# Four operand transposes of an attention block moved from TensorE to the DMA queue, three norms moved to TensorE, and a new order table

## The chip, the cores and the metric

One NeuronCore of a Trainium2 chip runs the whole program. The metric is the time of one execution in microseconds (us) of device time; lower is better.

## The reference

Three blocks follow each other. `q`, `k` and `v` have 2 batches, 8 heads, 768 rows and 64 columns.

```
q_bits, k_bits = (q @ proj > 0), (k @ proj > 0)        # 6 bits each
mask   = bucket(q_bits) == bucket(k_bits)
scores = where(mask, q @ k.T / 8, -1e9)
attn   = softmax(scores);  x = attn @ v                # -> 1536 tokens x 512
h      = max(x @ w1, x @ w2, x @ w3);  x1 = h @ w_out  # d_ff 768
g      = elu(x1 @ w_in);  out = g @ w_out2             # d_ff 2048
```

## The kernel before, in words

Everything is float32 outside and split inside into pairs of float16 numbers (a high and a low part), so that each product is three float16 matmuls.

The attention is cut into 6 chunks of 256 query rows (3 per batch), each chunk into 4 head pairs (a unit, u = 0 to 23), each unit into 4 tiles of 128 query rows of one head (t = 0 to 95). For a tile TensorE makes 8 score matmuls into PSUM ring `s` (2 buffers, L621), VectorE takes the row maximum (L624) and two small factors (L625, L627), ScalarE the exponential (L629). In the units of the first chunk (u < 4) the probabilities stay float32: TensorE turns them in the same `s` buffer (L641), they are copied to SBUF (L645), and TensorE multiplies with v (L650). From u = 4 on they are split into two float16 parts (L658 or L660, then L664) and turned by a DMA (`PT<-hl`, L666), before 18 matmuls with v (L672 to L674).

`plan_qk` prepares k for each head pair (u = 0 to 3 and 12 to 15: 12 blocks of 128x128) and q for each two pairs of a chunk (every even u: 8 blocks). Its steps are: load (L388), a norm, two small instructions that make a power of two out of it (L318, L320), scaling (L396 on ScalarE or L397 on VectorE), the high part (L398, VectorE), the low part (L400, GpSimd or VectorE), transposes of the pairs on TensorE into a PSUM buffer `mo` (L410, for k in two groups of six) with a copy to `ka` or `qa` by ScalarE or VectorE (L413), a DMA that moves one half to `kb` or `qb` (L417), the projection for the bits (L429 or L431), the bits (L441), their transposition (L445, L453 to L457) and small DMAs that put them behind the halves (L464). The scores of a unit wait for all of that.

The norm is made in one of two ways. `square` has ScalarE square and sum (L333, an ACTIVATE and a read of the accumulator), `gram` has TensorE multiply each 128x128 block of upper bfloat16 halves with itself (L297) and VectorE take the maximum (L301). Both end in two matmuls with one column (L280, L281). Before the change `gram` serves q of u = 0 and k of u = 0 and 1.

Beside the first tiles the weights of the second block are converted (`dc2w`, `w`; L531 to L560), and v is (L492 to L502). The second block's matmuls (L713) begin when the first chunk is finished; the third block (L713 with `win`, L848) fills the second half of the time.

The order of the work is not made by a loop: each operation is put into a list with the engines that could do it, and the table `ORDER`, a compressed string, names for each place which operation is emitted there, and on which engine. Each engine works its instructions off in that order, so that one that waits holds up all behind it on its engine. DMAs are issued from SyncE's queue (SP) or ScalarE's (ACT). Engine letters in the table are PE, V (VectorE), A (ScalarE), G (GpSimd), D (SP).

Of the kernel before, what the change touches and what calls it, by code (L numbers as in the profile page):

```python
# [30 lines left out]
class Graph:  # L31
# [73 lines left out]
    "c-lQyOITXx))u_6@y5m*8*gm9vC$at$|h<6O~OWvfLG8cV48~QKx_wMG7y`A*bKyzf!Gejb|AI`@pK@z1F;>5?LbTiVmlB|2I9#;Ob3#a|9Sqk&H4Yezi)l-`>uDb4UgNcWz6SqKV$!(5=mvVN=j#N"  # L105
    "UYZxbaC_pfyb0VH#K#-Q{hL!L@yD)|EQI>ufz@F1o3Y)KSzPaUb6yn;&OCQ6#%A5uPUiA=F1Li6?m6)kt}A@s`|GDDxx3zQy0__k`*)Pktj44}ISg~}>3gp*<Qw!iGxo@|sC-`@Q!JXP_>nHIxOP*_"
    "Roys4;5BgO2-XzyrGa()oa>XK<R4~Lxc8|EI}ljad@;UnBlI%6^yj&H^Wo2!Qu8#Vo)4?^$Ajj`nQkc>NxwSwYa@oM^Xr)5<jv$~%S=CJet`#PhOHjtEoUn5s|h=ro!;|W@x8w$dEq%b?pO%!FK+mj"
    "jf9(3>+yuV&Mn`%EOrszj_*Z&R52#^FqUg;o{R3!U?F@3f8jFCi@%xwT^e?~E`Ih{CB%yjw?`r;HWya+13O+)9Xi;FD%7^{*}KR~Dzc`~z0$Q`gmw)Rp)0fPa^eU3kMZ}D_9eH>G2==2O1Y#N_D(NQ"
    "{-3qR1fAm-<E+zVUNIRQJF5tSPPn6-#a_?GyKM}!e7MHlfvrioIT+fb7@H?ZU;;hWJ?C4mt+orZpp1;$ncFtw<+JpFSRDMFm<%bcClb6`T6JbmVE&tOIQ7WV(BJ3^3sVZe4L;_e;zK$1Lmh4ttHao-"
    "?r68UmJ`Jd5!Ibqk(n2qpcb^!_PJO{WD|xB&z72xH_uRW#4X{!u*Rp5W&E4f8O9g07oIP#7ffC+xv8jq=kr^acNEcp?ZA$IKzVx}bx8c%OI$vGqMMu}V&*?wYf|r}L+&<DM?P$L3|k4#^*LqdKUC`Y"  # L110
    "{DrS$g0ZmfUqt+i+(2&}^Bu$z74DgD#;K##F{AER+s2=p>|=v#-C~b8u$?yx*XB~+p`P)I`60@6ZT@PlKKlANwu2oEBH@2du+YeN=Letr&-wlUH;DYAeSWkWGf3WFGxwJni70YLoJ;WqvPvm8Cs;jG"
    "u9Nyp<;=gltn?Wl6^ifdeu*02vV!7uJ}P)A(XeJqi3u4z0^vneY%W~2oeerJS9F}c=>N=zH>AIj2xYE4vu<PW7XQGVE{q5WKln*m?V!@Fx3x#tf+}KW)lk>zF?oNSQ^n-I!*lP1ukA;FLhM4ecN}+r"
    "rRr2O77w)J2KFoD^|fuAnH1JU%zr7OcE|1l#nmNr8e*1$;32YfJ@qwOhHbDI<Hu7z;j`!3H}8?nIrO{8DHpzNU?Q*`3|c-HXvLQXGr^YDJr}LTIkM#=Wq^0}x;d!F(2!bcJrPXcx~i>X$(eyvp4jRa"
    "?c#sQm~Ot=bB<3Kl(UKJ-m~x3Z^hAtS*iB#tr*vK&M-Vnm}Y#4O}*L~CMPdDf8oSmFzhn61Djp=fd5X^uDTX2PM7?Lr*5xlL352TeLd@b>t5TijdieWN71ykxlK>!>%lGmJa)ueuf@6B$G9R;y&Q=6"
    "ep4*`b?6Tkm=glgnCHM-7Sd|0val^;bg^cLZ^CtRzRk<%?>jNc-uGOk{67?5_f=e$q*XD-5t+^SD)gu2h4x5fus>CE-<;}H)V8s7))ZJ-Fld6WywheZv}S&c=t?KX7mgE7BGu98GIBM(_(eQ68<E<k"
    "#N?TBaR#L@caLz@BQ`9$PnW$O-bVEAt@G%Vv#xnLcI?@Zc)ZVizMh>IyK!cGkM$dlV*A=@gW2jhy>#L`zZ^xUeiE}yJFaWH)pl)XeEEmsvi8p0@5JswobeLj3jTSF%tzLJ{=hZk5Yc7-u@a7Oc?cd|"
# [53 lines left out]
TR = lambda blocks: (0, 625, 142 * blocks)  # L170
# [803 lines left out]
```

## Time and profile before

| | |
|---|---|
| median of 3 runs | 646.44 us (646.3 to 650.33) |
| the profiled execution's own time | 646.06 us |
| its span, first to last instruction | 644.3 us |
| TensorE busy | 624.7 us (97%) |
| VectorE busy | 528.0 us (82%) |
| ScalarE busy | 454.8 us (71%) |
| GpSimd busy | 218.5 us (34%) |

A time is one execution on the chip. The span lies inside it; 1.76 us of the profiled execution are around it. Busy is the union of the instructions of an engine. Engines overlap, so shares do not add up, and a share is a mean over stages that have different limits.

### The profile page before, as it was taken

To read this page: it belongs to the slowest core of one execution; us is meant where nothing else is said; L and a number is where in the kernel's file an instruction comes from. 1 tells how busy PE (TensorE), PEld (TensorE's weight loads), DVE (VectorE), ACT (ScalarE), POOL (GpSimd) and SP (SyncE) were. 2 spreads that over 40 slices of the span, in tenths; PEclk is the share of its full clock that TensorE was granted. 3 is DMA by queue.
4 is the path that set the end of the run, shared out by engine and by line. 5 is a ranking of instruction groups with operands and counts; after the bars stand their busy time and mean duration, and the time that the engine had idled before them with its cause. 6 is when DMAs were issued, how large, how long until landed. Compare 5 with 4: busy or idle time off the path is not lost.

```text
span 644.3 us, 16489 instructions
## 1 busy us (share of the span) xinstructions
PE 624.7 (97%) x6414; PEld 490.8 (76%) x6414; DVE 528.0 (82%) x1493; ACT 454.8 (71%) x858; POOL 218.5 (34%) x196
## 2 busy tenths in 40 slices
PE   4999889999999999999999999999999999999997
PEld 4788768888888888888888887766676666667664
DVE  6899999998878988898765898888888676887564
ACT  3899999999878777866635878866755665554431
POOL 1210175756656474575631101112111221120021
PEclk9999989999999999999999999999999999999999
DMA  8775699979799777888666634231302100000022
GB/s 261 200 242 152 180 202 229 217 131 218 150 189 178 149 156 164 174 169 151 147 132 218 181 96 128 68 99 35 97 19 71 45 1 2 1 1 2 1 92 105
DMA packets 176030, 81.35 MB, mean 126 GB/s; under 512 B 142672, under 2 KB 170320, under 8 KB 175952
## 3 DMA queue, kind: packets, MB, share of 16 engines
q1 hardware_dynamic: 171678, 75.54, 50.3%
q10 hardware_dynamic: 4274, 4.76, 2.6%
q8 instruction: 50, 0.82, 0.6%
q14 instruction: 28, 0.23, 0.1%
HBM read 38.80 MB, written 3.15 MB: 65 GB/s over the span
## 4 chain that ended last, share of the span: by engine, by line
PE 80%; DVE 4%; ACT 4%; DMA 3%; issue 1%; POOL 0%; DVEq 0%; SPq 0%; ACTq 0%
PE mo L713 47%; PE out L848 19%; PE s L621 6%; PE o L672 2%; PE o L673 2%; PE o L674 2%; ACT P L629 1%; DVE m L624 1%; DMA kb<-ka 1%; DMA rawv<-in_v_dram 1%; PE mo L410 1%; DMA PT<-hl 1%; ACT hl L645 1%; DVE hx L734 0%; ACT mo L535 0%
## 5 line engine op out<-in xcount | busy, mean ns | idle before, releaser
L713 PE MATMUL mo<-xT,w 128*128 128x256 f16 x1296 | 152.6, 272 | 0.0
L664 POOL TENSOR_TENSOR hl<-P,hl 128x768 f16<-128x768 f32 x69 | 115.0, 1674 | 64.9 <-ACT hl L658 31.5
L713 PEld LDWEIGHTS <-w 128*128 128x128 f16 x1296 | 123.6, 98 | 16.7
L713 PE MATMUL mo<-x1T,win 128*128 128x256 f16 x1152 | 135.8, 273 | 0.0
L848 PE MATMUL out<-wo2t,gt 128*128 128x512 f16 x576 | 134.9, 379 | 0.0
L713 PEld LDWEIGHTS <-win 128*128 128x128 f16 x1152 | 112.3, 98 | 24.2
L629 ACT ACTIVATE P<-s,bias,scale 128x768 f32<-128x768 f32 x96 | 94.6, 991 | 28.8 <-DVE bias L627 17.6
L841 POOL TENSOR_TENSOR gt<-g,gt 128x256 f16<-128x256 f32 x57 | 39.3, 695 | 213.2 <-ACT gt L839 125.4
L624 DVE TENSOR_REDUCE m<-s 128x1 f32<-128x768 f32 x96 | 91.1, 951 | 12.6 <-PE s L621 11.2
L848 PEld LDWEIGHTS <-gt 128*128 128x128 f16 x576 | 54.9, 97 | 52.7
L832 ACT ACTIVATE r<-mo,nih 128x256 f32<-128x256 f32 x96 | 44.8, 469 | 69.1 <-PE mo L713 65.0
L835 DVE TENSOR_SCALAR uu<-e,sg 128x256 f32<-128x256 f32 x96 | 35.5, 371 | 26.3 <-ACT e L834 25.7
L658 ACT CAST hl<-P 128x768 f16<-128x768 f32 x62 | 50.7, 830 | 2.9 <-DMA PT<-hl 2.4
L672 PE MATMUL o<-vt,PT 128*128 128x65 f16 x480 | 51.3, 193 | 0.2
L673 PE MATMUL o<-vt,PT 128*128 128x64 f16 x480 | 51.3, 194 | 0.0
L674 PE MATMUL o<-vt,PT 128*128 128x65 f16 x480 | 51.1, 192 | 0.0
L837 DVE SCALAR_TENSOR_TENSOR g<-mo,aj,uu 128x256 f32<-128x256 f32 x96 | 46.1, 482 | 6.0 <-POOL gt L841 2.0
L621 PE MATMUL s<-ka,qa 128*128 128x384 f16 x192 | 48.1, 332 | 2.5 <-ACT P L629 1.9
L621 PE MATMUL s<-kb,qb 76*128 76x384 f16 x192 | 48.2, 332 | 1.0 <-DMA kb<-ka 1.0
L672 PEld LDWEIGHTS <-PT 128*128 128x128 f16 x480 | 44.4, 96 | 2.7 <-DMA PT<-hl 0.4
L673 PEld LDWEIGHTS <-PT 128*128 128x128 f16 x480 | 44.3, 97 | 2.1
L713 PEld LDWEIGHTS <-wot 128*128 128x128 f16 x432 | 41.4, 98 | 5.6
(212 smaller groups left out, 1158.7 us busy)
## 6 DMA issues: line engine op xcount, KB each, us to landing
raww<-in_moe_w_dram SPq DMA_DIRECT2D x17, 512.0 KB
raw<-in_moe_w_in_dram SPq DMA_DIRECT2D x14, 512.0 KB
raw<-in_moe_w_out_dram SPq DMA_DIRECT2D x13, 512.0 KB
rawk<-in_k_dram SPq DMA_DIRECT2D x8, 384.0 KB
raww<-in_moe_w_out_dram SPq DMA_DIRECT2D x6, 512.0 KB
out_dram<-ot SPq DMA_DIRECT2D x12, 256.0 KB
rawq<-in_q_dram SPq DMA_DIRECT2D x10, 256.0 KB
wot<-in_v_dram SPq DMA_DIRECT2D x4, 384.0 KB
```

The costliest lines, as they stand in the source:

```text
L621: PE.matmul(ps.ap[:, h, :NK], lh[0:n, h0 + i, j], rh[0:n, i, h * CH:(h + 1) * CH], start=first, stop=not first)
L624: op({"V": vred(S)}, lambda e: V.tensor_reduce(out=m.ap, in_=ps.ap[:, :, :NK], op=ALU.max, axis=AX.XY), rd=[ps], wr=[m], prio=t + 80.5)
L629: op({"A": act(S, ap=2, acc=int(u < FU)) - 42}, lambda e: A.activation(out=P.ap.rearrange("p (c n) -> p c n", c=2), in_=ps.ap[:, :, :NK], ...
L658: A.copy(hl.ap[:, 0], P.ap)
L664: op({"G": gtt(S), "V": (vtt(S), -109.46)}, lambda e: eng[e].tensor_tensor(out=hl.ap[:, 1], in0=P.ap, in1=hl.ap[:, 0], op=ALU.subtract), r ...
L672: PE.matmul(oo, pt.ap[:, kt], vt.ap[:, i, kt, :D + 1], start=(kt == 0), stop=False)
L673: PE.matmul(oo[:, :D], pt.ap[:, kt], vt.ap[:, i, kt, D + 2:], start=False, stop=False)
L674: PE.matmul(oo, pt.ap[:, NS + kt], vt.ap[:, i, kt, :D + 1], start=False, stop=(kt == NS - 1))
L713: PE.matmul(o, lh(kk, x), rh(kk, y), start=(kk == 0 and pi == 0), stop=(kk == n - 1 and pi == 2))
L832: op({"A": act(NQ, ap=1) - 42}, lambda e, m=m, o=o, r=r: A.activation(out=r.ap, in_=o.ap[:, :NQ], func=AF.Relu, scale=nih.ap[:, m:m + 1]), ...
L837: op({"V": vstt(NQ)}, lambda e, m=m, o=o, uu=uu, gg=gg: V.scalar_tensor_tensor(out=gg.ap, in0=o.ap[:, :NQ], scalar=aj.ap[:, m:m + 1], in1= ...
L848: PE.matmul(outs[j].ap, gt.ap[:, x, j * 128:(j + 1) * 128], wo2t[f].ap[:, y], start=(len(seen) == 1 and pi == 0), stop=(len(seen) == n and ...
```

## The change

For `0 < u < 4` (k of u = 1, 2 and 3, and q of u = 2) one DMA issued from SP turns all blocks, from `nat` straight into `ka` or `qa`. The TensorE transposes and the copies out of PSUM fall away there. For all `u < 4` the norm is made by `gram`; new to it are k of u = 2 and 3 and q of u = 2. Two estimates of a DMA cost on the ACT queue are one higher in the list, which no instruction shows. `ORDER` is replaced.

```diff
 ORDER = (
...
-        x2 = norm2([(raw, fl)], N, prio, u < 1.007, acc, True, [s, inv])
+        x2 = norm2([(raw, fl)], N, prio, u < 4, acc, True, [s, inv])
...
         nb_ = nt // 2 if nt > 8 else nt
-        for c in range(nt // nb_):
+        if 0 < u < 4:
+            op({"D": TR(nt)}, lambda e: SP.dma_start_transpose(out=ta.ap.rearrange("p h s t -> p (h s) t"), in_=nat.ap.rearrange("p n t d -> p (n t d)")),
+               rd=[nat], wr=[ta, tb, bits], prio=prio)
+        for c in range(nt // nb_ if not 0 < u < 4 else 0):
             ps = mo()
```

The two tables unpack to lists of 3359 and 3352 places. Read as lists, they stand so (the number is the place):

```
                                        old place        new place
scores of tile 0, PE                    108              106
exponential of tile 0, A                126              128
exponential of tile 21, A               529              516
first matmul of the second block, PE    539              540
k u=1: transposes | DMA transpose       80, 88 PE        101 D
       bits matmul, PE                  122              122
q u=2: transposes | DMA transpose       101 PE           118 D
       bits matmul, PE                  185              169
k u=2: transposes | DMA transpose       154, 179 PE      176 D
       bits matmul, PE                  189              198
k u=3: transposes | DMA transpose       231, 254 PE      282 D
       bits matmul, PE                  275              312
       half to kb, D                    367              331
       scores of tile 12, PE            390              381
low parts (L400): k u=1, q u=2, G       63, 90           69, 116
places on PE, V, A, G, D                694 1488 776 181 218   690 1508 775 155 222
```

Between the exponentials of tile 0 and of tile 21 ScalarE has 90 places in the old list and 85 in the new one. Kind by kind the new list has there: three `square`s of k fewer and one of q more (k's are that of u = 3, which `gram` makes now, and those of u = 13 and 14, which come later; q's is that of u = 10, which comes earlier); two scalings of k (L396) more and one of q more; three copies to `ka` (L413) fewer; two casts L658 fewer; and one L535 more, one L539 and one turn of k's bits (L457) fewer. Ahead of tile 0 it has one `square` of k and one of q, one copy to `ka` and one to `qa` and one write of v fewer, one scaling of q and two conversions (L539, L543) more, and two loads of v there in place of one weight load. A load of q (for u = 4) is issued from ScalarE's queue at place 123, behind the `square`s and ahead of k's scaling (126) and tile 0's exponential; it waits until the low part of q u=2 (place 116) has been made, for the buffer.

Between the maxima of tiles 0 and 21 VectorE has 178 and 174 places. The new list has there: two scalings of k and one of q (L397) fewer, one copy to `ka` fewer, two L546 and one L560 fewer, one L502 fewer, one write of v fewer; and one each more of L436, L441, L455, a turn of k's bits, and L660. Ahead of tile 0 it has three L301 more, for the new `gram`s (one behind the scores of tile 0 in the list, all ahead of its maximum), one write of v and one L546 more, and one copy to `ka`, one scaling of q and two conversions fewer.

On SP the new DMA transposes have behind them: k u=1: two weight loads; q u=2: `kb<-ka` of k u=1 and a load of v; k u=2: a load of k for the second batch and one of weights; k u=3: one of weights and one of q.

## Rows read from the trace of the kernel before

**Rows 1.** Busy time by stretches; columns PE, PEld, DVE, ACT, POOL, clock, DMA share, GB/s

```profile
0.00:20.00 20.00, 11.09 (x144) 9.55 (x145) 13.60 (x51) 9.36 (x18) 4.34 (x17) 1.00 0.71 224
20.00:90.70 70.70, 64.87 (x669) 54.95 (x667) 66.77 (x192) 67.93 (x121) 16.46 (x13) 0.98 0.73 203
90.70:140.00 49.30, 48.90 (x675) 41.51 (x675) 48.16 (x130) 49.02 (x78) 31.20 (x21) 1.00 1.03 201
140.00:640.00 500.00, 499.41 (x4932) 384.80 (x4930) 398.20 (x1124) 328.48 (x644) 166.46 (x146) 1.00 0.45 104
```

**Rows 2.** The chain that ended last, 0 to 105 us: start, us, what

```profile
60.60 6.27 DMA kb<-ka
...
89.67 0.98 ACT P L629
...
91.50 1.31 PE mo L713 x12
```

**Rows 3.** ScalarE instructions by line, 0 to 100 us: count, busy us, mean ns, idle before

```profile
L658 ACT CAST hl<-P 128x768 f16<-128x768 f32 x6 | 4.9, 830 | 0.1
...
L413 ACT COPY ka<-mo 128x768 f16<-128x768 f16 x6 | 4.8, 809 | 0.9 <-PE mo L410 0.9
L333 ACT ACTIVATE junk<-rawk 128x768 bf16<-128x768 f32 x5 | 4.2, 842 | 0.0
...
L333 ACT ACTIVATE junk<-rawq 128x512 bf16<-128x512 f32 x5 | 3.2, 634 | 0.1
...
L333 ACT ACTIVATION_READ_ACCUMULATOR junk<-rawk 128x1 f32 x5 | 1.0, 201 | 0.0
...
L396 ACT ACTIVATE rawk<-rawk,sk 128x768 f32<-128x768 f32 x1 | 0.9, 935 | 0.0
...
L396 ACT ACTIVATE rawq<-rawq,sq 128x512 f32<-128x512 f32 x1 | 0.7, 719 | 0.0
```

**Rows 4.** VectorE instructions by line, 0 to 100 us

```profile
L546 DVE SCALAR_TENSOR_TENSOR dc2w<-mo,dc2w 128x512 int32<-128x512 int32 x18 | 12.3, 683 | 0.0
L560 DVE SCALAR_TENSOR_TENSOR w<-dc2w,swm,w 128x512 f16<-128x512 f32 x14 | 10.5, 760 | 0.1
...
L301 DVE TENSOR_REDUCE gm<-mo 128x1 f32<-128x128 f32 x12 | 3.4, 284 | 4.9 <-PE mo L297 3.8 <-PE mo L281 1.0
...
L502 DVE SCALAR_TENSOR_TENSOR vt<-wot,vs,vt 128x768 f16<-128x768 f32 x3 | 3.0, 1008 | 0.0
...
L397 DVE TENSOR_SCALAR rawk<-rawk,sk 128x768 f32<-128x768 f32 x4 | 2.5, 613 | 0.0
...
L413 DVE COPY ka<-mo 128x768 f16<-128x768 f16 x2 | 1.1, 552 | 0.3 <-PE mo L410 0.3
```

**Rows 5.** ScalarE in order of time: two neighbours, start and duration

```profile
26.05 0.80 ACT L645 COPY hl<-s 128x768 f32<-128x768 f32 x1
26.75 1.00 ACT L629 ACTIVATE P<-s,bias,scale 128x768 f32<-128x768 f32 x1
```

**Rows 6.** TensorE by line and shape, 0 to 20 us

```profile
L410 PE MATMUL mo<-ident,natk 128*128 128x128 f16 x24 | 3.0, 311 | 0.0
...
L297 PE MATMUL mo<-rawk 128*128 128x128 bf16 x12 | 1.6, 306 | 1.7 <-DMA rawk<-in_k_dram 1.7
```

**Rows 7.** The same, 20 to 60 us

```profile
L410 PE MATMUL mo<-ident,natk 128*128 128x128 f16 x24 | 2.0, 219 | 0.0
```

**Rows 8.** DMA transposes of the tile `PT`, 60 to 135 us: issue time in ns, min/median/max

```profile
L666 SPq DMA_TRANSPOSE PT<-hl x16: 1368/1432/2630, 86.2 to 134.5; - x16
```

**Rows 9.** The chain that ended last, whole span: a DMA transpose from issue to landing

```profile
121.62 5.03 DMA PT<-hl
```

**Rows 10.** In order of time, 0 to 30 us: small DMAs, the scores behind them, a subtraction

```profile
17.38 1.60 SPq L464 DMA_DIRECT2D kb<-btk  x2
...
17.89 1.15 POOL L400 TENSOR_TENSOR natq<-rawq,natq 128x512 f16<-128x512 f32 x1 [1.62 <-DVE natq L398]
...
20.91 0.84 PE L621 MATMUL s<-kb,qb 76*128 76x384 f16 x2
```

More of the change, by code (lines that the diff above doesn't have):

```diff
@@ L109 @@
[L109 to L116, printed above, removed]
@@ L149 @@
[L149 to L152 removed]
+    "c-k#iOH?A))&@icL<M|N_$+);XxkRPD13sC=3y%!+CbY1Xm^V@12Gwhe+J^ppfMSUoq?DP#PmQ+55#03b_U|@e=RY0ASMIx-hVAI8HmY1Oa@{y_;=a&t2*a=``h2%r>NppK@)w7OXVt^iS>5Dy=<N5"
@@ new lines @@
+    "d42xC?~QzPJ9xc6#SUUgTtNvF@`y^u+&`YRA94Fl4(r0%0)l$n%ic@v55N9elTZuL+c#{Q$->)@vh77Y_wuJVm?L}~^~S>U$wrs;iZit-qf>Rp?~$_4kG^y`U0rv9;8kepXxTcY(ynol<F>CIA=c$O"
+    "W^yLZCSB8s<R|DJPW|hMCc+8U%DP|9@SSt%>Ig?5L)QI5x4&pRs5P(3HNImGKYG6H7Y6qJgP>nq;uqL{5Rb=XM~N~~7h4t&seiU7F`om+8i-RvOc4{|NAbj+(VDR1XJt}{Q!1y#=Z_m%-uFGnD(kE+"
+    "`BsrId}dv6Mzwn(yD6sP#9d2w<{j<LXG_+Vu*vGR*k`r3_GMrHr!>dRl6QX2<R7)WKVSAPE&6<n#Q<k{#gFKBQ0$fDP2e-{?Ut9i>-+K`5@h(N5>l=rfGC6^3bTldbP3<7bce!-sX{rcik-&Z+1OaW"
+    "NP<Oq@26&Q^Md=+c)#RklJD`N`y2a&{xG~5!;YvC>5esOzhIum7KV}%>L-iD<xRKS<DGNiOVatz{xp6Wms>Y(RZQI<hr9lG#3PHwzBAi;{_z9v`je#iihCT53FLR>@wLPat@f4YuRE8QSmn&6__llq"
@@ new lines @@
+    "!qRUB=%+hslyBx@68|}h1+TB($-1p=xGb>ryJdYUW_S2+ok~Y&kskj!JojGj+CT4~PAaHTwa6V{?BQ{S{zPjc*zyF2_S%|MD`-)@G%`8^_fyk#cr)qz+KqgncDb>qyDJu^cExT8P0!YQ!;T+Wk;z;m"
+    "v7S?8m8&+KXI{T?C&-y&=r4YIzvkjj30-rmGhYbB2<rdFWv}^jUF<doBpzpQZHqd46p2Rm|7TlLCJ09+S~vJ_V`y{=!|~hgm5um?j2e2s`_Z?@Kl)!;wqwi?ck%NTkA3FK+cR_aNASqu+z&?=Bg@`|"
+    "FR55^>Zqo}?@yUqikRd$8vpe;da1nGO~n4@CE~YK<Tb^39MxRJg<lhx>VI{2H+QC_AZqZX{5-W|n<~R_f~{cAmZ4gTb^4tscExqDwj>Glf|2%d@_oP-bh<K@4nHMUzEW=wO$T$`o=_NDaIqOY3Ug`w"
+    "#Q2JvJNky>5Af?}(X-$$$m%M={~Z-~hu1d(9{zz`wSTDJH&6Ic>}XqZ>^y6AZtjL7(Tm7sq&6D63cbC-K1w7db1q3_;a_e~z3lw@)1EaC<;NtQwc)lTb3M1n<;m$+-fuT<sPkI{^UC=BA94j{h8g30"
@@ new lines @@
+    "9RFe6e^ZgmQT}bUZ|^xB2p`3C%EJhX&F@CP`*mh<Tl)FgfkduKcFBV0vb!%E(C*VKUMv*WQ^HD<E}r=5<cEI!k<nzmqfN~@=*JdkH0CNynO?HH+#-A}WB)aAWwDnr<f|*(^^difKdAny;*jwto=6fi"
+    "{7>ec0oU2WFQdor6}xVS&@q?$2ELY7e%HG_Yr#bmg?U@go&4hLCWOTJzO{daC@kX3>u)GRRX8HgJ$uVx@pOC<f-Yc^*r>bzw>4$G-iUf?ZC$^4t#)i(yeX^qD>od0KM4yS2qw?tdZTX3dPwaN?%9pA"
+    "%&G4zk<sXU%y|{sw!1#EY}(uWuXtVI9~{n`zht-Fj>Y~!FyuzyYjb@W?hStQdQk=+sQB(a9sT;}O=Ru!z|9>+r2SIPbna^K{Y3^LKQo+%L+X=PE33$iE#-vo^T(ax$Qj$d?so+)_y4U6{Ce#UCpeMl"
+    "*H2e2?!3N>xjPrUUgK{RCKsVZCxxHvQrG`{dvKXZQW;!s8I~b#n7Y7Q!&(!AYemqby<3i5q1*^<U$Ok+89v&k!$!ZKou9)kt{l7d4}r|&vi%)epOQGb6s->DqEiFcEONwezSu0<#Mj`}xL@Bb27)OS"
@@ L153 @@
+    "j+w@Q!wE^V@hQyrFpiHw)zha&C^VTZ7W31m&;iC%z&J?bqZa7@)G|5_nQ^lHs0HY#WfbC32mqs_qff`lg3)_sAsML8$as7dOrw)PpFMl_^qJ)uiKn2FvBg53&ql42&&EfeSpm<i&&D8O9kp3)wr3WY"
+    "V78Dtd0Ho|R-4rdGDtRH6BD)x5?0$Y8)+qD>x&np0AylvV$w!>tTrHEyEjctOoBdXv%#1IJb(Ut^7%cRc=7y$F!}t&1jrK;&nI5KeEIyvb1QgXKL3ChWC567z&_6>$^6TgFGx%QpPG6x_59@&DNMcq"
+    ">%{YWkxacHWmqS{NuKvAIZu(rFJFEz0{$P1=?$#"
 )
@@ L416, in plan_qk @@
         all_ = lambda t: t.ap.rearrange("p h s t -> p (h s) t")
-        op({"D": (475, 450, 1200 * (1 if kind == "k" else 0.75)), "A": (520, 460, 1200 * (1 if kind == "k" else 0.75), 341.16)}, lambda e: dq(e).dma_start(
+        op({"D": (475, 450, 1200 * (1 if kind == "k" else 0.75)), "A": (520, 460, 1201 if kind == "k" else 901, 341.16)}, lambda e: dq(e).dma_start(
             out=all_(tb)[0:64], in_=all_(ta)[hs * 64:hs * 64 + 64]), rd=[ta], wr=[tb], prio=prio + 433.29)
```

74 lines of the change are left out of this document (33 added, 41 removed).

## The prediction

> **What bounds the kernel now.** I read the stretches first, then the chain, then the lines of the engines in the stretch that the change is in.
>
> The stretches [rows 1] show three stages. From 140 to 640 us TensorE is busy for 499.41 of 500 us and works off a list; the end can come earlier there only if this stage starts earlier or has less in it. From 20 to 90.7 us TensorE is idle for 5.83 us, while ScalarE is busy for 67.93 and VectorE for 66.77 of 70.70 us. From 90.7 to 140 all three are above 97%. In the first 20 us nothing is full: TensorE 11.09, VectorE 13.60, ScalarE 9.36. The chain [rows 2] says the same: it runs through an exponential of ScalarE until 90.65 us, and from 91.50 on through TensorE's L713. So what an instruction of ScalarE or VectorE is worth depends on its place: ahead of tile 0 (some 20 us) little, between tile 0 and tile 21 (whose exponential is the one at 89.67 us) its whole time, if both engines lose it.
>
> **The change part by part.**
>
> *Removed from ScalarE and VectorE, added to them.* Places between tile 0 and tile 21, old list to new list, at the durations of [rows 3]: three squares of k fewer, each 0.842 + 0.201, make -3.13; one of q more, 0.634 + 0.201, +0.83; two scalings of k, +1.87, and one of q, +0.72; three copies to `ka`, -2.43; two casts, -1.66. ScalarE's sum is -3.8 us. One instruction more and two fewer are left out; the two conversions among them have about one length. For VectorE by [rows 4]: two scalings of k, -1.23; one of q, two thirds as long, -0.41; one write of v, taken like a scaling, -0.61; the copy, -0.55; L502, -1.01; two L546, -1.37; one L560, -0.76; together -5.9. The five that come in have lengths between L301's 0.284 and the copy's 0.552, so +1.4 to +2.8; I take 2.0, since three of them are tiny. VectorE's sum is -3.9 us. Durations overlap on an engine: an L645 of 0.80 is followed by the next start after 0.70 us [rows 5], a factor of 0.875. That makes **-3.3 us** for ScalarE and -3.4 for VectorE. Both are full in this stage, and both have to reach tile 21, so the gain is the smaller of the two. The three new L301 (0.85 us) come ahead of tile 0's maximum, where VectorE has 6.4 us idle; there I cost them at nothing, at 0.85 if that cover is gone.
>
> *TensorE.* 44 transposes go: 12 of k and 8 of q in the first stretch at 3.0/24 = 0.125 us [rows 6], 24 of k at 2.0/24 = 0.083 [rows 7], together 4.5 us. 16 `gram` matmuls come, at 1.6/12 = 0.133 each [rows 6], 2.1 us. The net of -2.4 us lies in stretches where TensorE waits anyway [rows 1], so it is no term of the sum; it is cover for what is late.
>
> *DMA transposes.* The kernel of before already turns 12 blocks with one DMA, for `PT`. SP spends 1.43 us to issue one [rows 8], so four cost SP at most 5.7 us (q has 8 blocks). Behind each stand loads of weights, q or v and, for q u=2, the half of k u=1, all used dozens of places later; I put their delay at 0. The path of k or q gets another length: low part, issue, landing, then the bits matmul of TensorE, which stands in order ahead of tiles' work. How long is that? The nearest rows: small DMAs whose issue ended at 18.98 us had landed when the scores read them at 20.91, so 1.9 us at most [rows 10]; a `PT` transpose took 5.03 us from issue to landing in a stretch where the DMA engines are full [rows 9, 1]; a half of 192 KB took 6.27 behind two weight loads [rows 2]. In the first 90 us the DMA share is 0.72, not 1.03, so I take the middle of 1.9 and 5.03, **3.5 us**, and keep 1.9 to 6.27 for the range. What the order leaves for it: 539 places take 91.5 us, 0.17 us each; from DMA transpose to bits matmul there are 21, 51, 22 and 30 places (k u=1, q u=2, k u=2, k u=3), so 3.6, 8.7, 3.7 and 5.1 us. With 3.5 us all four are hidden, the first and third barely.
>
> A rule of the Trainium skill speaks against this edit: *VectorE: DVE Perf Modes*, "The three transpose paths", gives 390 ns for a 128x128 transpose on TensorE and 1309 ns for one through the DMA crossbar, and advises TensorE. By 1309 ns a block, an estimate, 12 blocks would be 15.7 us, three of the four would come some 11 us late, and the time would be near 680 us. The row disagrees: 12 blocks in 5.03 us are 0.42 us a block [rows 9].
>
> *Waits added.* ScalarE's load of q waits for a subtraction on GpSimd; k's scaling and tile 0's exponential are queued behind it. GpSimd's step is 1.15 us [rows 10] and ScalarE is idle half of the first 20 us: 0, at most 1.15.
>
> *A wait that may go.* TensorE's tile 12 stood on the half of k u=3 [rows 2], whose copy came 23 places ahead of it; now there are 50. ScalarE was busy meanwhile, so I count nothing and leave up to 1 us for the range.
>
> *The rest of the order* is shuffled too, and 26 places net go from GpSimd, some to VectorE. From 140 us on VectorE is at 398 of 500 us and TensorE is what is full, which hides it; if TensorE were idle there for 1% it would cost 5 us, as bound.
>
> **The sum.** 646.06 (the profiled execution) - 3.3 = **642.8 us**. The median of the runs, 646.44, lies 0.4 above the profiled execution, which is small beside the range.
>
> **The rivals.**
>
> *The early relief counts too.* If the stage is one chain of ScalarE, the squares of k and q and the copy that go ahead of tile 0 (1.04 + 0.83 + 0.81, times 0.875, 2.3 us) bring tile 0 forward as well: 640.5, and 639.5 with the wait of tile 12. For it: the last 20 us of the chain ahead of 90.7 are ScalarE's. Against it: ScalarE is idle for more than half of the first 20 us [rows 1], so something else sets when tile 0 starts.
>
> *The gain is swallowed.* The stage from 90.7 to 140 has ScalarE at 49.02 of 49.30 us, and of the three squares of k only that of u = 3 is gone; two, 2.09 us, are put off behind tile 21. Times 0.875 they give back 1.8 of 3.3 us: 644.6; if L502 and the write of v that VectorE puts off (1.6 us) count too, near 646. For it: all three engines are full there. Against it: in the new list a square of q and other conversions come earlier in exchange.
>
> *Slower: the DMA transposes land late.* Transposes queue behind loads, TensorE stands at the bits matmul, and the tiles' turns behind it starve ScalarE. With L from issue to landing the stalls are (L - 3.6) + (L - 3.7) + (L - 5.1) where positive; they eat the whole 3.3 us at L = 5.3. At the 6.27 us of the half [rows 2] they are 6.5 us: 646.1 - 3.3 + 6.5 = 649.3. For it: `PT`'s 5.03 is near the turning point. Against it: that row is from a fuller stretch, and TensorE's idle 5.83 us and its 2.4 us less work take a part. The skill's 1309 ns is this rival at its extreme; by the row I give it no chance of its own above 0.01.
>
> **How the numbers follow.** Forecast 0.54, early relief 0.17, swallowed 0.19, late 0.10. A measurement of this kernel tells about 1%, 6.5 us, from no change. Faster by more than that, under 640.0 us, is half of the early relief and a tail of the forecast: 0.16. Slower by more, over 652.9, is the far tail of the late landings and of an order that leaves TensorE idle after 140 us: 0.06. Within 1%: 0.78. The range reaches from the early relief, 639.5, to the near part of the late landings, 647.5.
>
> **What would show it.** Right: the exponential of tile 21 and the first L713 some 3 us earlier than 89.67 and 91.50; no L333 of k or q ahead of tile 0; ScalarE and VectorE still full between; TensorE full from 140 us on to an end 3 us earlier. The DMA transposes would show in SP's order with about 1.4 us each, and TensorE's waits would name none of them. Wrong: waits of L429 on `ka` from a DMA, of microseconds; the first L713 as late as before; or TensorE idle behind 140 us.

## The result, and the profile after

The change makes the kernel slower: 655.09 us (median of 4 runs, 652.25 to 659.92) against 646.37 for before beside it, ratio 1.0138 (95% interval 1.0097 to 1.0178). Run again later as `after_again`, the same kernel took 652.79 us (7 runs), ratio 1.0100 (1.0065 to 1.0135). The profiled execution took 654.88 us, its span 653.1.

The code moved down by 3 lines: L621, L629, L713 of before are L624, L632, L716. In the experiments all lines are up to 4 less than that; L712, L713, L715 and L716 are one and the same line.

First the stretches of after, with the columns of [rows 1], and the last one new:

```profile
0.00:20.00 20.00, 10.52 (x136) 8.57 (x136) 12.34 (x50) 8.44 (x15) 3.08 (x16) 1.00 0.74 236
20.00:90.70 70.70, 63.77 (x647) 54.33 (x648) 65.67 (x193) 64.36 (x114) 17.17 (x14) 1.00 0.78 214
90.70:140.00 49.30, 48.46 (x645) 40.27 (x643) 47.87 (x123) 47.37 (x74) 29.51 (x21) 0.97 0.90 195
140.00:640.00 500.00, 494.09 (x4924) 382.06 (x4921) 401.75 (x1140) 334.39 (x651) 139.87 (x120) 1.00 0.45 104
640.00:653.10 13.10, 8.60 (x44) 4.02 (x42) 5.78 (x13) 1.30 (x3) 0.67 (x1) 1.00 0.21 81
```

From 20 to 90.7 us ScalarE is busy 3.6 us less than in [rows 1] (64.36 of 70.70), as the change intends, and yet the stage ends hardly earlier. The surprise is the fourth row: TensorE, which had been idle for 0.59 us of 500, is idle for 5.91.

Two stages can be told apart by the first matmul of the second block (first xT row) and of the third (x1T row). The view of L713 or L716 by its operands (count, ns min/median/max, first and last start in us, forms), of before:

```profile
L713 PE MATMUL mo<-xT,w x1296: 269/272/274, 91.3 to 387.2; 128*128 128x256 f16 x186
L713 PE MATMUL mo<-x1T,win x1152: 269/273/273, 374.1 to 632.4; 128*128 128x256 f16 x192
```

of after:

```profile
L716 PE MATMUL mo<-xT,w x1296: 269/272/421, 92.2 to 395.3; 128*128 128x256 f16 x186
L716 PE MATMUL mo<-x1T,win x1152: 269/273/273, 382.3 to 640.6; 128*128 128x256 f16 x192
```

and of `after_again`:

```profile
L716 PE MATMUL mo<-xT,w x1296: 269/272/274, 91.0 to 392.1; 128*128 128x256 f16 x186
L716 PE MATMUL mo<-x1T,win x1152: 269/273/273, 379.0 to 637.3; 128*128 128x256 f16 x192
```

I call the time up to the first one the start, between them the middle, and from the second to the end of the span the rest. Before: 91.3, 282.8, 270.2. After: 92.2, 290.1, 270.8. `after_again`: 91.0, 288.0, 270.9. So the start is as long as before instead of 3 us shorter, and the middle, which the forecast left alone, is 5.2 to 7.3 us longer. Most of that is waiting: in the middle TensorE is idle for 6.8 us in after and 5.7 in `after_again`, against 1.0 before. The middle of before, of after and of `after_again`, with the columns of [rows 1]:

```profile
91.30:374.10 282.80, 281.81 (x3687) 242.89 (x3685) 239.49 (x625) 220.98 (x357) 154.65 (x106) 1.00 0.84 173
...
92.20:382.30 290.10, 283.34 (x3672) 242.12 (x3670) 242.52 (x626) 224.34 (x364) 136.72 (x95) 1.00 0.79 169
...
91.00:379.00 288.00, 282.35 (x3673) 241.68 (x3670) 242.19 (x627) 224.71 (x364) 138.20 (x95) 1.00 0.82 170
```

The two executions of one kernel differ by 2.1 us in the middle, 1.7 of them ahead of the 25th exponential, a stretch that in after begins at a lower clock (last section).

In the start, the chain of waits of after:

```profile
19.80 6.34 DMA ka<-natk
26.14 0.05 issue
26.18 1.12 PE mo L432 x36
```

This is the DMA transpose of k's second pair (u = 1), 6.34 us from issue to landing, and the bits matmul (before's L429) behind it. TensorE waits for it 1.1 us, and 1.4 in `after_again`, where it lands after 6.60. No wait of TensorE names the other three transposes.

In the middle, TensorE's waits from 106 to 400 us (us in total, times, longest). Before has two, together 0.8 us. After:

```profile
PE s L624 <- ACT P L632: 3.1, 4, 1.2
PE o L675 <- DMA PT<-hl: 1.5, 2, 1.0
PE mo L448 <- ACT hx L739: 1.1, 1, 1.1
PE mo L413 <- DVE hx L741: 0.2, 1, 0.2
```

TensorE waits for ScalarE: scores for an exponential that still holds their buffer, and bits behind a copy of the second block. The first of these waits ends at 142.20 us. VectorE's instruction that this exponential needs:

```profile
139.60 0.20 DVE L630 TENSOR_SCALAR bias<-m,scale 128x1 f32<-128x1 f32 x1
```

and ScalarE in order of time:

```profile
139.43 0.72 ACT L561 ACTIVATE wot<-dc2w,osc 128x512 f16<-128x512 f32 x1
140.04 0.61 ACT L746 CAST hTb<-hx 128x512 f16<-128x512 f32 x1
140.55 0.73 ACT L561 ACTIVATE wot<-dc2w,osc 128x512 f16<-128x512 f32 x1
141.17 1.86 ACT L632 ACTIVATE P<-s,bias,scale 128x768 f32<-128x768 f32 x2
```

The factor is there at 139.80, the exponential starts at 141.17: ScalarE has no gap in between, it works off conversions for the second block that stand ahead in its queue. Other waits begin further back. The copy that the bits wait for until 219.13 us stands behind a cast that waits for a `PT` transpose; the exponential that the scores wait for until 242.56 us (1.2 us) itself waits for GpSimd's subtraction:

```profile
217.75 0.83 ACT L661 CAST hl<-P 128x768 f16<-128x768 f32 x1 [1.60 <-DMA PT<-hl]
...
241.52 0.99 ACT L632 ACTIVATE P<-s,bias,scale 128x768 f32<-128x768 f32 x1 [1.44 <-POOL hl L667]
```

### The profile page after: what moved, and what is told of

Its sections match the earlier page's. It is cut to its first block, busy times and chain, and to the rows that moved or that the text cites. A ratio compares the mean times of both kernels' runs of the same rounds, so it can differ in the third digit from the quotient of the medians.

```text
span 653.1 us, 16389 instructions
## 1 busy us (share of the span) xinstructions
PE 625.4 (96%) x6386; PEld 489.3 (75%) x6386; DVE 533.4 (82%) x1513; ACT 455.9 (70%) x854; POOL 190.3 (29%) x170
## 4 chain that ended last, share of the span: by engine, by line
PE 75%; DVE 9%; DMA 7%; ACT 6%; issue 2%; SPq 1%; POOL 1%; DVEq 0%; ACTq 0%; POOLq 0%
PE mo L716 42%; PE out L851 19%; PE s L624 6%; DMA PT<-hl 3%; DVE m L627 3%; ACT P L632 2%; PE o L675 2%; PE o L676 2%; PE o L677 2%; DMA ka<-natk 1%; DMA rawk<-in_k_dram 1%; DMA raww<-in_moe_w_dram 1%; DMA rawv<-in_v_dram 1%; ACT hl L648 1%; ACT mo L538 1%
## 5 line engine op out<-in xcount | busy, mean ns | idle before, releaser
L716 PE MATMUL mo<-xT,w 128*128 128x256 f16 x1296 | 154.0, 273 | 0.0
L716 PEld LDWEIGHTS <-w 128*128 128x128 f16 x1296 | 123.9, 98 | 18.8 <-issue 1.1
L667 POOL TENSOR_TENSOR hl<-P,hl 128x768 f16<-128x768 f32 x65 | 108.8, 1682 | 94.9 <-ACT hl L661 54.1
L716 PE MATMUL mo<-x1T,win 128*128 128x256 f16 x1152 | 135.9, 273 | 0.0
L716 PEld LDWEIGHTS <-win 128*128 128x128 f16 x1152 | 112.1, 98 | 23.8
L632 ACT ACTIVATE P<-s,bias,scale 128x768 f32<-128x768 f32 x96 | 94.5, 989 | 23.9 <-DVE bias L630 15.4
L627 DVE TENSOR_REDUCE m<-s 128x1 f32<-128x768 f32 x96 | 90.9, 949 | 11.3 <-PE s L624 11.1
L844 POOL TENSOR_TENSOR gt<-g,gt 128x256 f16<-128x256 f32 x44 | 31.3, 714 | 232.6 <-ACT gt L842 123.5
L661 ACT CAST hl<-P 128x768 f16<-128x768 f32 x67 | 55.0, 827 | 10.5 <-DMA PT<-hl 10.0
L624 PE MATMUL s<-ka,qa 128*128 128x384 f16 x192 | 48.0, 332 | 6.5 <-ACT P L632 5.5
L624 PE MATMUL s<-kb,qb 76*128 76x384 f16 x192 | 48.4, 333 | 0.0
L716 PEld LDWEIGHTS <-wot 128*128 128x128 f16 x432 | 41.4, 98 | 5.6
```

Of the source, the lines that this page charges most:

```text
L624: PE.matmul(ps.ap[:, h, :NK], lh[0:n, h0 + i, j], rh[0:n, i, h * CH:(h + 1) * CH], start=first, stop=not first)
L627: op({"V": vred(S)}, lambda e: V.tensor_reduce(out=m.ap, in_=ps.ap[:, :, :NK], op=ALU.max, axis=AX.XY), rd=[ps], wr=[m], prio=t + 80.5)
L632: op({"A": act(S, ap=2, acc=int(u < FU)) - 42}, lambda e: A.activation(out=P.ap.rearrange("p (c n) -> p c n", c=2), in_=ps.ap[:, :, :NK], ...
L661: A.copy(hl.ap[:, 0], P.ap)
L667: op({"G": gtt(S), "V": (vtt(S), -109.46)}, lambda e: eng[e].tensor_tensor(out=hl.ap[:, 1], in0=P.ap, in1=hl.ap[:, 0], op=ALU.subtract), r ...
L716: PE.matmul(o, lh(kk, x), rh(kk, y), start=(kk == 0 and pi == 0), stop=(kk == n - 1 and pi == 2))
```

## The experiments

Two theories stood at first. *Two places*: the loss is the late first transpose, plus a later order that makes TensorE wait, whatever the operations. *The edit*: the DMA transposes and the new norms do the harm themselves. A third was added later: *the fit*: a table is fitted to its operations, and any disturbance costs.

All runs, with the ratio to before on the same chip (before's median there was 646.4 to 647.25); start, middle and rest are of the profiled execution. That is one execution, and not always a typical one: it is the fastest of `transposes_only` (4.1 us below the median) and the slowest of `edit_old_order` and `edit_old_tail` (3.4 and 3.0 us above).

| kernel | median us (runs) | ratio, 95% interval | start | middle | rest |
|---|---|---|---|---|---|
| before | 646.4 (23) | 1 | 91.3 | 282.8 | 270.2 |
| after | 655.09 (4) | 1.0138 [1.0097, 1.0178] | 92.2 | 290.1 | 270.8 |
| after_again | 652.79 (7) | 1.0100 [1.0065, 1.0135] | 91.0 | 288.0 | 270.9 |
| edit_old_order | 651.58 (12) | 1.0079 [1.0052, 1.0106] | 96.6 | 286.4 | 270.1 |
| order_alone | 657.10 (6) | 1.0156 [1.0105, 1.0207] | 98.6 | 286.7 | 270.8 |
| new_head_old_tail | 651.05 (12) | 1.0068 [1.0040, 1.0096] | 93.5 | 286.2 | 270.1 |
| old_head_new_tail | 658.67 (6) | 1.0179 [1.0137, 1.0221] | 96.0 | 290.8 | 270.7 |
| norms_only | 650.19 (12) | 1.0056 [1.0035, 1.0076] | 93.8 | 283.1 | 270.4 |
| transposes_only | 650.84 (12) | 1.0058 [1.0034, 1.0082] | 92.6 | 282.2 | 270.1 |
| k1_by_tensore | 651.19 (12) | 1.0063 [1.0035, 1.0090] | 89.5 | 288.1 | 270.8 |
| edit_blended_order | 652.32 (6) | 1.0088 [1.0056, 1.0120] | 98.1 | 284.7 | 270.2 |
| k1_tensore_old_tail | 655.84 (4) | 1.0142 [1.0115, 1.0169] | 88.6 | 295.5 | 270.1 |
| edit_old_tail | 657.90 (6) | 1.0179 [1.0154, 1.0205] | 95.7 | 293.3 | 270.1 |
| k1_tensore_old_order | 652.42 (6) | 1.0096 [1.0071, 1.0121] | 94.0 | 286.6 | 270.1 |
| k1_tensore_repaired | 651.75 (6) | 1.0077 [1.0053, 1.0101] | 92.8 | 286.8 | 270.1 |
| jitter_before | 657.87 (4) | 1.0171 [1.0148, 1.0195] | 102.6 | 283.4 | 270.1 |
| jitter_before_small | 650.09 (12) | 1.0043 [1.0024, 1.0062] | 91.5 | 284.6 | 270.1 |
| jitter_later_before | 668.77 (6) | 1.0350 [1.0319, 1.0380] | 91.1 | 306.1 | 270.1 |
| jitter_after | 679.91 (6) | 1.0503 [1.0453, 1.0552] | 114.1 | 289.9 | 270.8 |
| norms_moved | 648.04 (12) | 1.0015 [0.9993, 1.0038] | 93.1 | 283.4 | 270.4 |

**Edit and order apart.** The edit with the old table, before's operations with the new one, and two joints of the tables. The lists differ so (place in the old or the new list, engine):

```diff
 edit_old_order: the old list
-80, 88 PE    k u=1 transposes, with their copies 94 V, 95 A
+80 D         k u=1 DMA transpose (q u=2, k u=2, k u=3 likewise)
-84 A         square, k u=2
+84 PE, V     gram and reduction (q u=2, k u=3 likewise)
 order_alone: the new list, all of this undone in place
 new_head_old_tail: the change; new list to place 520, old list behind
 old_head_new_tail: before; old list to place 539, new list behind
```

> The change's own operations, placed in the order table of before (a DMA transpose where the first TensorE transpose of that load stood, the norm's matrix product and its reduction where the square stood). Two-place theory: about 5.3 us of the loss are TensorE's idle time in 140-640, and they come from the new order of the later work, so here that idle falls under 2 us and the time is 645 to 650. Rival, the edit itself disturbs the DMA queues and the engines throughout: 652 to 656, with 5 us or more of idle in 140-640.

> The operations of before in the order table of after (TensorE transposes and copies where the DMA transpose stands, the square where the norm's reduction stands). Two-place theory: idle of TensorE in 140-640 stays at 4 to 6 us although nothing is transposed by DMA, and the time is 649 to 655. Rival, the edit itself: within 1% of before, 645 to 650, with under 2 us of idle there.

> The change's operations; the new order up to place 520 (the exp of tile 20, some 89 us), the order of before from there on. Two-place theory: the idle in 140-640 falls under 2 us and the time to 649-651, what is left over before being the first stage. Rival, the edit: 653 to 656, as after.

> The operations and order of before up to the first matmul of the gated layers (place 539), and from there on the new order. Two-place theory: 650 to 653, with 4 to 6 us of idle in 140-640. Rival, the edit: as before, 645 to 648, with under 2 us.

The new order behind place 539 makes before's own operations 1.8% slower, and the whole new order 1.6%. There it has the waits of after, with nothing of the edit in the kernel. The scores' wait, TensorE in order of time, of after:

```profile
142.20 0.48 PE L624 MATMUL s<-ka,qa 128*128 128x384 f16 x2 [1.10 <-ACT P L632]
...
219.13 0.22 PE L448 MATMUL mo<-ident,bitsq 128*96 128x128 f16 x1 [1.08 <-ACT hx L739]
```

of `order_alone`:

```profile
146.53 0.48 PE L620 MATMUL s<-ka,qa 128*128 128x384 f16 x2 [1.09 <-ACT P L628]
...
223.03 0.22 PE L444 MATMUL mo<-ident,bitsq 128*96 128x128 f16 x1 [1.14 <-ACT hx L735]
```

and of `old_head_new_tail`:

```profile
146.05 0.48 PE L620 MATMUL s<-ka,qa 128*128 128x384 f16 x2 [1.09 <-ACT P L628]
```

The scores' wait stands 48 to 50 us behind the first matmul of the second block in all three, 1.1 us long. In both, the same six instructions of ScalarE stand between a cast and this exponential as in after. The edit as the cause of these waits has fallen. The middle of `order_alone` is 3.9 us longer than before's, against 5.2 in `after_again`, so what is left over is not attributed. Both kernels lost more than expected, though: `order_alone` in its start (98.6), `old_head_new_tail` also at its joint, where TensorE waits 2.7 us for VectorE's bits. But `edit_old_order` and `new_head_old_tail` missed their numbers too: TensorE is idle for 3.5 and 3.1 us in 140-640, not under 2, and waits 2 us for `PT`. And a joint makes waits of its own: in `new_head_old_tail` TensorE stands at it, 82 to 106 us, behind a norm whose reduction VectorE reaches late.

```profile
PE mo L279 <- DVE gm L300: 3.5, 1, 3.5
```

**Parts of the edit.** `norms_only` and `transposes_only` take the old table, `k1_by_tensore` the new one; `edit_blended_order` passes from the new to the old table between places 450 and 600.

```diff
 norms_only
-        x2 = norm2([(raw, fl)], N, prio, u < 1.007, acc, True, [s, inv])
+        x2 = norm2([(raw, fl)], N, prio, u < 4, acc, True, [s, inv])
 transposes_only: the change without that line
 k1_by_tensore, against after
-        if 0 < u < 4:
+        if 1 < u < 4:
...
-        for c in range(nt // nb_ if not 0 < u < 4 else 0):
+        for c in range(nt // nb_ if not 1 < u < 4 else 0):
```

> The order table of before; of the change only the norms: three squares of ScalarE replaced by TensorE's product and VectorE's reduction, all operands of k and q still transposed by TensorE. If the loss that remains under the old later order (4.65 to 5.2 us) comes from the transposes' landing times: 645 to 648, about as before. Rival, the norms load VectorE and TensorE in the first stage: 649 to 652.

> The order table of before; of the change only the four DMA transposes, the norms as before. If late landings (6.3 us instead of the 3.5 of the prediction) cost the first stage its time: 649 to 652, with a wait on the transpose of k's second pair before 35 us. Rival, the norms are the cost: 645 to 648.

> The change in its own order table, but k's second pair (the first of the four DMA transposes, 6.34 us) is transposed by TensorE and copied by ScalarE and VectorE again. If its late landing takes back the first stage's gain: the wait of TensorE near 26 us goes and the time falls 1.5 to 3 us, to 652 to 653.5, the later idle staying. Rival, that landing is hidden and only the later order costs: 654 to 657.

> The change's operations; the order of after at the start, carried over into the order of before between places 450 and 600 step by step instead of at one cut, so that the 3.5 us that TensorE waited at the cut (for the norm of a gated layer's weights) are gone. If the edit itself is worth about nothing: 646 to 648.5. Rival, the edit costs 4 to 5 us whatever the order: 650 to 652.

Both halves of the edit cost about the same, 0.56% and 0.58%, so neither expectation told them apart (the profile of `transposes_only` is its fastest execution, 646.71 us, and shows too little of its cost). At least part of the cost is where they stand in the list. In `transposes_only` the first transpose was expected to be waited for before 35 us; no wait names it. But it stands on SP ahead of the small DMAs with the first pair's bits, and TensorE's first scores wait for these. SP's queue, in order of time:

```profile
16.82 1.54 SPq L405 DMA_TRANSPOSE ka<-natk  x1
18.47 1.60 SPq L466 DMA_DIRECT2D kb<-btk  x2
```

and TensorE:

```profile
21.75 0.80 PE L623 MATMUL s<-kb,qb 76*128 76x384 f16 x2 [3.56 <-DMA kb<-btk]
```

The wait is longer than the delay: before's scores on `kb` came at 20.91 [rows 10], 0.8 us earlier, since TensorE was transposing until then. `edit_old_order` has the same wait, 3.3 us; after's new list issues those small DMAs first (17.57 against 19.80 us), and has none. Where the rest of the 3.9 us that `transposes_only` loses lies is not shown, since the execution with the profile hardly lost any. The blend missed; its joint had a wait of 2.5 us, again.

`k1_by_tensore` is the useful one, since it differs from after in nothing but the first transpose. It came out a little below its 652 to 653.5, and TensorE's wait near 26 us is gone. The exponentials, in order of time, of `after_again`:

```profile
41.84 0.99 ACT L632 ACTIVATE P<-s,bias,scale 128x768 f32<-128x768 f32 x1
...
88.34 0.97 ACT L632 ACTIVATE P<-s,bias,scale 128x768 f32<-128x768 f32 x1
...
104.68 0.98 ACT L632 ACTIVATE P<-s,bias,scale 128x768 f32<-128x768 f32 x1
```

and the same three (the 6th, the 20th, which is tile 21, and the 25th) of `k1_by_tensore`:

```profile
40.42 0.99 ACT L631 ACTIVATE P<-s,bias,scale 128x768 f32<-128x768 f32 x1
...
86.95 0.97 ACT L631 ACTIVATE P<-s,bias,scale 128x768 f32<-128x768 f32 x1
...
103.31 0.96 ACT L631 ACTIVATE P<-s,bias,scale 128x768 f32<-128x768 f32 x1
```

Each comes 1.4 us earlier, at 40 us as at 104: a loss taken once and carried along, and as large as TensorE's wait of 1.4 us. (The first two exponentials are 1.7 us later in `k1_by_tensore`; its clock was 0.63 from 20 to 25 us.) The medians differ by 1.6 us (652.79 and 651.19), though their intervals overlap. The middle is the same, 288.0 and 288.1.

**The joint, and a control.** The first two use the new list to place 520 and the old one behind, with what the new list puts off left late; the third the old table. The control changes no operation.

```diff
 k1_tensore_old_tail: k1_by_tensore, new list to 520, old list behind
 edit_old_tail: the whole change, joined the same way
 k1_tensore_old_order: k1_by_tensore in the old list
 jitter_before: before
-place p
+place p + r, r random within 4, for 60 <= p < 520; engines kept
```

> The change, but k's second pair transposed by TensorE; the order of after up to place 520, that of before behind it, with the operations that the new order had put off left as late as it has them, so that nothing piles up at the joint. If the loss is the sum of the late landing (3.9 us by k1_by_tensore) and of the new later order: both are gone, and the first stage's gain of some 2.5 us is left: 642 to 645.5, faster than both kernels. Rival, any order but the one fitted to before's operations costs 3 to 5 us: 649 to 652.

> The same joint of the two orders with the whole change, k's second pair by DMA. If the late landing costs 3 to 4 us in any order: 3 to 4 us above k1_tensore_old_tail, 646 to 649. If the landing mattered only through the new later order: within 1 us of k1_tensore_old_tail.

> The change without the DMA transpose of k's second pair, in the order table of before throughout. Against edit_old_order (651.58): if the late landing is what the edit costs, 647 to 648.5; if the old order's misfit with the new operations is, 650 to 652.

> A control: the operations of before, none changed, in the order of before with every place from 60 to 520 (some 15 to 89 us) shifted by a random amount of up to 4 places, engines kept. If the order table is fitted so closely that any disturbance of it costs what these hybrids cost: 649 to 652. If small shifts are harmless: 645 to 648, and the costs measured for the hybrids belong to their edits.

All four came out above the ranges expected of them. The control decides how the others are to be read. With before's own operations, 385 of 3359 places taken by another operation, it loses 10.6 us, as much as the worst hybrid with the edit (`edit_old_tail`, 10.7). It loses them in the start (102.6), where TensorE is busy for 63.38 of 70.70 us, at a lower clock:

```profile
20.00:90.70 70.70, 63.38 (x606) 54.55 (x603) 58.52 (x167) 58.60 (x107) 8.79 (x8) 0.93 0.59 173
```

The whole start, of before and of `jitter_before`:

```profile
0.00:91.30 91.30, 76.56 (x813) 64.88 (x814) 80.96 (x242) 77.89 (x140) 20.93 (x30) 0.98 0.73 208
...
0.00:102.60 102.60, 84.43 (x814) 71.19 (x815) 82.75 (x245) 79.67 (x141) 20.65 (x30) 0.92 0.65 187
```

It is 11.3 us longer; for 3.4 of them TensorE is idle more, and for 7.9 it is busy longer with the same work, so the lower clock has the larger part. The shifts are one random draw, so 10.6 us is one example and not a mean.

So what an edit costs in an order that was not fitted to it says little of the edit. Only pairs that share an order can be read: `k1_tensore_old_tail` and `edit_old_tail` differ by 2.1 us for the first transpose, `k1_tensore_old_order` and `edit_old_order` by -0.8; the intervals of either pair overlap. The joint had a fault here as well: the transfer of a half of q had been put off while the scores had not.

```profile
PE s L623 <- DMA qb<-qa: 4.4, 1, 4.4
```

**How sharp the fit is.** I formed the third theory here: the tables are fitted, the loss of after is the difference of two fits, and neither the edit nor the order alone carries a price. Each of the shifted tables is again one random draw.

```diff
 k1_tensore_repaired: the transfer of q's half back at its old place
 jitter_after: after, places 60 to 520, r within 4
 jitter_before_small: before, places 60 to 520, r within 1.5
 jitter_later_before: before, places 540 to 1500, r within 4
```

> k1_tensore_old_tail with its joint repaired: the put-off transfer of q's half (waited for 4.4 us) and the matmuls and additions back at the places of before, only VectorE's and ScalarE's preparatory work left late. If the joint was what hid the gain: 655.84 - 4.4 = 651.4 or less, down to 645. If an order that isn't fitted costs its 5 to 10 us wherever it is joined: 652 to 657.

> The kernel after, its places 60 to 520 shifted at random by up to 4, as in jitter_before. If the new table is fitted to its operations as closely as the old one was: 660 to 666. If it is a loose fit, so that after's loss is a table no better than a disturbed one: 653 to 658.

> The kernel before, places 60 to 520 shifted by up to 1.5 only (50 places change within an engine's own queue). If the loss grows with the size of the shift: 647.5 to 651. If any shift at all costs the whole: 654 to 659.

> The kernel before, its first 540 places untouched, places 540 to 1500 (some 90 to 260 us) shifted by up to 4. If the later part, where TensorE is the bound and its idle is 0.1%, is as sensitive as the first: 650 to 656, with 3 us or more of TensorE's idle in 140-640. If only the first stage is sensitive: 646 to 648, and the new later order's waits are its own.

`jitter_after` and `jitter_later_before` lost more than either of their ranges. After loses 25 to 27 us by shifts of the size that cost before 10.6. That speaks against after's table being a loose one, but it does not measure how closely it is fitted: of the 21.9 us by which the start is longer than after's, TensorE is idle for 7.5 and busy longer for 14.4, and the clock stood at its lower level from 90 to 114 us.

```profile
90.00:100.00 10.00, 10.00 (x53) 8.96 (x53) 6.22 (x18) 6.27 (x10) 1.83 (x2) 0.50 0.17 52
```

With before's operations the loss grows with the shift (3.2 us for 1.5 places). The middle is as sensitive as the start, although TensorE had been idle there for only 0.59 us of 500: with an untouched start it loses 21.9 us for 960 shifted places, against 10.6 for the 460 of `jitter_before`. Among its waits, 106 to 400 us, those for exponentials are of after's kind, only more of them; the other two shown are not among after's:

```profile
PE s L620 <- ACT P L628: 7.7, 8, 1.6
PE mo L430 <- ACT qa L412: 4.3, 2, 4.1
PE mo L279 <- ACT btq L452: 1.1, 1, 1.1
```

The repaired joint gave back most of what its wait had cost, 4.1 of 4.4 us, and landed between its two ranges; it is no faster than `k1_by_tensore`.

**The last two.** After once more, and `norms_only` with one product moved.

```diff
 norms_moved, places in the old list
-84 PE, V     gram and reduction, k u=2
-99 PE        sum, k u=2
+88.5 PE      gram, behind k u=1's transposes (80, 88)
+98.5 V       reduction, behind k u=1's copies (94, 95)
+101.5 PE     sum, behind q u=2's transposes (101)
```

> The kernel after, unchanged, in up to 12 executions. If the late landing of the first transpose costs 3.9 us: 653.5 to 656.5, above k1_by_tensore's 651.19. If the difference was the spread of four executions: 650.5 to 652.5.

> norms_only with TensorE's product for k's third pair moved behind the second pair's transposes, its reduction and the sum behind the copies that TensorE waited 2.1 us for. If that wait made the first exp late: the first exp comes back to 23-25 us from 27.07, and the time falls from 650.19 to 645-648.5. If not: 649 to 652.

After confirmed its loss, at the low end (1.0% against 1.4%) and between its two ranges. Moving three operations by some 2 to 15 places took 2.1 us off `norms_only` (the intervals just touch): the norms on TensorE now cost nothing that is measured. The first exponential is still at 26.41 us and not at 23 to 25, and 1.5 of the wait's 2.1 us are left. The two profiled executions differ by 0.4 us only, so where the 2.1 us were gained is not shown.

No kernel here beats before.

## Why the prediction was wrong

*The step that failed most* is "The rest of the order", costed at nothing. VectorE's slack (398 of 500 us) and TensorE's full list were taken as cover. They are none, because an engine takes its work in order, as ScalarE does in the rows at 139 to 141 us. What counts is not an engine's share but whether the one instruction that frees a buffer stands early enough in its queue. The middle became 5.2 to 7.3 us longer and the rest 0.6 to 0.7. The 5 us named as a bound for TensorE's idle time after 140 us were about what came, 5.3 and 3.8 us more than before, but they were not in the sum. Shown: the new later order has these waits with before's operations too, and an order shifted at random in the same stretch has more of them. Not shown: that the new operations need a worse later order. `norms_only`, `norms_moved` and `transposes_only` keep the old middle within 0.6 us in their profiled executions, but the five kernels with both parts and the old later order (the two with the faulty joint left out) have 284.7 to 286.8, 1.9 to 4.0 above before. A table fitted anew to the change with the old later part as its beginning was not tried.

*The second step* is the 3.5 us from issue to landing. The first transpose took 6.34 and 6.60, above the upper bound of 6.27. I had chosen by a mean: "In the first 90 us the DMA share is 0.72", and its lower end, 1.9 us, was of small DMAs with bits and not of 12 blocks. The transpose does not run in a mean. Where it runs, before's own windows have (last columns: clock, DMA share, GB/s)

```profile
20.00:25.00 5.00, 4.49 (x52) 3.02 (x50) 4.82 (x14) 4.74 (x8) 1.15 (x1) 1.00 0.92 257
25.00:30.00 5.00, 4.75 (x44) 4.24 (x43) 3.50 (x14) 3.87 (x10) 0.49 (x1) 1.00 1.01 296
```

so the full `PT` stretch [rows 9] was the nearer row, and those two windows were there to be asked for. The places left 3.6 us, so by the rival's formula (L - 3.6) TensorE should have waited 2.7 to 3.0 us; it waited 1.1 to 1.4, since the places are not of one length: without the wait the bits matmul would have come some 5.2 us after the issue, not 3.6. The rival *late* thus had the right mechanism for the first transpose only, at half its price; the stalls at the third and fourth (2.6 and 1.2 us at 6.27) did not come. *VectorE: DVE Perf Modes*, "The three transpose paths", of the Trainium skill gives 1309 ns for one 128x128 transpose through the DMA crossbar. As a price for each block of a larger DMA that is again not what the trace shows: 12 blocks in 6.34 us are 0.53 us each.

*The gain* fits its mechanism, though no run isolates it from the rest of the new order. ScalarE is busy 3.6 us less from 20 to 90.7 us in after (3.3 forecast). With the first transpose back on TensorE tile 21's exponential is at 86.95, 2.7 us before the 89.67 of [rows 2], of the 3.3 forecast, and the second block starts 1.8 us earlier (89.5). In after they are at 89.04 and 92.2, in `after_again` at 88.34 and 91.0. So the late landing took back about half of the gain. The other 0.7 us of after at tile 21 were not the clock's, which was 1.00 from 20 to 90 us; behind it, from 90.5 to 93.7, it was.

*The small terms.* The wait that may go went: `PE s <- DMA kb<-ka`, 1.0 us in before, is not among after's waits. TensorE's 2.4 us less work cannot be seen in its busy time, 625.4 us in after and 624.8 in `after_again` against 624.7, which also holds stretches at the lower clock. The load of q on ScalarE's queue did hold ScalarE up, for 1.5 us at 21.25 in after, but tile 0's exponential then still waited 0.4 us for VectorE, so it cost nothing there, as put down. SP's cost of issue was not 1.43 us for each: in after it was 1.57, 2.72, 1.39 and 2.35, and 5.18 for the third in `transposes_only`. That a transpose's place in SP's queue costs nothing held for the new list, where no wait names it; in the old one TensorE waited 3.3 to 3.6 us behind it.

*The chances.* Slower by over 1% had 0.06, named as "the far tail of the late landings and of an order that leaves TensorE idle after 140 us". It was mainly the second of these, and it deserved a rival of its own, with the waits for exponentials as its place.

## What to carry to other kernels

Where the order is a table, a replaced table can be the larger part of the change, even if the diff is about four operations: read the middle of the new list, engine by engine, for what stands ahead of each instruction that frees a buffer. A price measured by putting one table's work into another's order needs a control, and shifting the untouched kernel's order at random is a cheap one (several draws are better than the one taken here); without it I would have put 4 to 5 us down to the edit. Estimate a DMA's landing time from rows whose DMA share is that of the few us in which it will run, and not that of the stage.

## What was not expected of the hardware

TensorE's granted clock is a term of the time around the end of the start. In after it is 0.83 from 90 to 100 us (a mean; it is at 0.50, the lower of its two levels, 1.2 GHz, from about 90.5 to 93.7). In the 10 us ahead of that TensorE was busy for 7.69. `after_again`, the same kernel, has its 0.83 from 80 to 90 us, where TensorE is busy for 8.40 and waits 1.6 us for an exponential. After's window:

```profile
90.00:100.00 10.00, 9.94 (x93) 7.96 (x93) 9.15 (x20) 9.33 (x15) 6.04 (x4) 0.83 0.95 232
```

and the same of `after_again`:

```profile
90.00:100.00 10.00, 10.00 (x126) 8.42 (x124) 9.93 (x25) 10.00 (x15) 5.50 (x4) 1.00 0.83 221
```

93 recorded matmuls against 126 in 10 us. The 25th exponential comes at 107.56 us there against 104.68 here, 2.9 us for 0.7 at tile 21; how much of the 2.2 us between is the clock's is not separated. So two executions of one kernel differ here by what a whole edit was to bring. In `order_alone` the clock was at 0.50, the lower level, from 30 to 40 us, behind 8.13 busy of 10 us, and its start is 7.3 us longer than before's. In the starts of `jitter_before` and `jitter_after`, where the same matmuls run as in the kernels that they shift, TensorE's busy time grew by about twice what its idle time did (7.9 against 3.4 us, 14.4 against 7.5): the larger part of what these orders cost was not the waits themselves but slower matmuls.
